# Splitting 576 output columns 512+64 (504+72) instead of 288+288 in a two-layer attention and MLP kernel

## The chip, the cores and the metric

The kernel runs on one core of one Trainium2 chip. The metric is the device time of one execution in microseconds (us), lower is better.

Engine names in the profile: PE is TensorE (matmul), PEld its weight loads, DVE is VectorE, ACT is ScalarE, POOL is GpSimd, and SPq is the queue of SyncE, from which most transfers and all DMA transposes are issued here. The granted clock is the share of TensorE's full clock that the chip's throttle let through, as the profiler recorded it.

## The reference, cut to what matters

The input is 2048 rows of D = 576 columns. Two layers, each an attention block and an MLP, both with a LayerNorm in front and a residual sum behind:

```python
x = x + A(layernorm(x), wqkv, wo)          # 32 heads of 18, sliding window of 256
x = x + B(layernorm(x), w1, b1, w2, b2)    # 576 -> 4608 -> gelu -> 576
x = x + A(layernorm(x), wqkv, wo)
x = x + B(layernorm(x), w1, b1, w2, b2)
```

Three kinds of matmul end in 576 columns: the projections to q, k and v, the output projection `wo`, and the second MLP matmul `w2`. Matmuls write to PSUM, which this kernel uses in banks; none of its matmuls is wider than 512 columns, and each output of 576 columns is made by two matmuls in two banks.

## The kernel before

The program is laid out by a planner at build time. The kernel describes tasks (one engine, what they read and write, an assumed cost and latency in us); the planner repeatedly takes the task that can start first by its assumed times, and so fixes for each engine one static order of instructions. The waits between engines are added afterwards. An assumed time can therefore be wrong without making the result wrong, but it decides what stands in front of what.

Rows are handled in chunks of 4 tiles of 128. While the attention of one chunk runs (scores on PE, exponentials on ACT, masks on POOL, then P times V on PE), PE fills its gaps with matmuls of the previous chunk's MLP and of the next chunk's projections.

```python
def mm_cost(n):                                   # what the planner assumes of a matmul, us
    return max(n / 2400.0, 0.026) + (0.006 if n > 64 else 0.0)

def two_out(lhs, rhs, n, reads, prio, after=()):  # projections and output projection
    bs = [Bank(FILL), Bank(FILL)]                 # FILL = (6, 5, 4): PSUM banks
    for o in range(2):
        ...                                       # 5 matmuls of n = 288 columns into bs[o]

# second MLP matmul: per tile two outputs, each 18 matmuls in three indivisible blocks of 6
for hh in range(2):
    b = Bank(FILL)
    for f0 in range(0, NFH, 6):                   # NFH = 18
        ...
        add("pe", fn, ..., cost=6 * mm_cost(HB))  # HB = 288
    resid(t, hh, b, prio, ...)                    # DVE: x_res += PSUM

# after the attention of a chunk: transpose its output by DMA, then the output projection
for i in range(nt):
    add("sp", lambda e, i=i: e.dma_start_transpose(attT[...], attq[:, i, :]),
        ..., dma="t", ring=8, cost=1.3, lat=4.0, move=0.6, prio=prio - 0.1)
```

The softmax here doesn't subtract the row's maximum and nothing guards it: scores larger than these inputs give would overflow.

## Time and profile before

| | before |
|---|---|
| time, median | 987.56 us (3 runs, 985.93 to 987.72) |
| PE busy share | 96% |
| DVE, ACT, POOL busy share | 32%, 59%, 37% |
| mean granted TensorE clock, profiled run | 0.991 |

From the page of the kernel before: the busy time of each engine with its share of the span, and the chain that ended last, by engine.

```profile
PE 949.5 (96%) x9592; PEld 606.9 (61%) x9592; DVE 317.1 (32%) x772; ACT 586.0 (59%) x705; POOL 368.8 (37%) x507
PE 78%; DMA 5%; DVE 5%; POOL 5%; ACT 4%; issue 3%; DVEq 0%; POOLq 0%
```

PE is the bound: whatever leaves it idle, or lengthens what it does, costs time.

From the groups of the same page: source line, engine, operation, shapes out<-in, count, then busy us and mean ns of one, then the engine's idle time just before and what ended it.

```profile
L776 PE MATMUL ps<-w_sb,hT 128*128 128x288 bf16 x2304 | 316.1, 288 | 6.0 <-DVE x_res L709 4.9
L751 PE MATMUL ps<-xnTm,w_sb 128*128 128x512 bf16 x1440 | 319.4, 379 | 0.1
L709 DVE TENSOR_TENSOR x_res<-ps,x_res 128x288 f32<-128x288 f32 x160 | 70.7, 449 | 363.4 <-PE ps L776 342.6
```

L776 is the second MLP matmul, L751 the first, L709 the eviction that adds the second one's result to the residual. The 288 ns of one matmul is not its price, since matmuls overlap. The price is the distance between starts, which the timeline gives (start us, length us, instructions of one kind merged):

```profile
954.73 12.25 PE L751 MATMUL ps<-xnTm,w_sb 128*128 128x512 bf16 x56
966.81 17.80 PE L776 MATMUL ps<-w_sb,hT 128*128 128x288 bf16 x144
```

So 512 columns cost (12.25 - 0.379)/55 = 215.8 ns and 288 columns cost (17.80 - 0.286)/143 = 122.5 ns.

L601 are transposes of q and k, L722 those of the attention output, L558 and L564 projections and output projection:

```profile
288.72 3.58 SPq L601 DMA_TRANSPOSE kT<-qn  x1
292.40 5.19 SPq L722 DMA_TRANSPOSE attT<-attq  x4
...
294.20 0.65 PE L558 MATMUL ps<-wqkv,xnTa 128*128 128x288 bf16 x4
294.69 0.29 PE L564 MATMUL ps<-wqkv,xnTa 128*128 128x288 bf16 x1
295.55 0.67 PE L558 MATMUL ps<-wo_sb,attT 128*128 128x288 bf16 x4 [0.57 <-DMA attT<-attq]
```

### The profile page before, as it was taken

The numbers are of one execution on the slowest core, as the hardware profiler recorded it, in microseconds if no ns is written. First come the engines' busy times: TensorE is split into PE (matmuls) and PEld (weight loads), VectorE is DVE, ScalarE is ACT, GpSimd is POOL, SyncE is SP. The second block draws the span as 40 slices with busy tenths as digits, with TensorE's granted clock in tenths as the row PEclk, the third lists the DMA queues.
The fourth block names the chain that finished last, engine by engine and source line by source line (L and its number), as shares of the span: only waits on it lengthen the run. The fifth ranks groups of instructions, "written<-read, shape, count | busy, mean of one in ns | idle before, by whom it ended". The sixth has DMA issues, their size and how long they took to land.

```text
span 987.9 us, 22924 instructions
## 1 busy us (share of the span) xinstructions
PE 949.5 (96%) x9592; PEld 606.9 (61%) x9592; DVE 317.1 (32%) x772; ACT 586.0 (59%) x705; POOL 368.8 (37%) x507
## 2 busy tenths in 40 slices
PE   8898889999999999999999999999999999999998
PEld 6665547655575656756476565756567564657556
DVE  5653612722145211534028130361115310132001
ACT  0476676377753777447761777627774487852531
POOL 4555725334333434325153252433333352531000
PEclk9999899999999999999999999999999999999999
DMA  9846380964269250881529542494516816084540
GB/s 195 173 116 136 74 253 15 208 174 138 68 145 192 60 178 28 188 187 34 191 56 204 136 126 80 133 170 106 169 49 167 177 44 198 14 220 118 172 132 25
DMA packets 227287, 129.58 MB, mean 131 GB/s; under 512 B 141808, under 2 KB 225008, under 8 KB 227184
## 3 DMA queue, kind: packets, MB, share of 16 engines
q1 hardware_dynamic: 217872, 120.43, 49.4%
q0 software_dynamic: 6880, 5.03, 2.7%
q10 hardware_dynamic: 2432, 2.65, 0.9%
q8 instruction: 76, 1.25, 0.5%
q14 instruction: 27, 0.22, 0.1%
HBM read 90.69 MB, written 2.36 MB: 94 GB/s over the span
## 4 chain that ended last, share of the span: by engine, by line
PE 78%; DMA 5%; DVE 5%; POOL 5%; ACT 4%; issue 3%; DVEq 0%; POOLq 0%
PE ps L776 29%; PE ps L751 27%; PE ps L558 7%; PE ps L675 7%; PE ps L628 6%; ACT pT L637 3%; POOL pT L658 2%; DMA attT<-attq 2%; DVE x_res L709 2%; PE ps L564 2%; POOL rstd L499 2%; DVE st_all L486 2%; DMA x_res<-in_A_x_dram 1%; DMA kT<-qn 1%; DVE xn L509 1%
## 5 line engine op out<-in xcount | busy, mean ns | idle before, releaser
L637 ACT ACTIVATE pT<-ps 128x1024 bf16<-128x1024 f32 (+2 forms) x384 | 347.2, 971 | 128.1 <-PE ps L628 126.9
L658 POOL TENSOR_SCALAR_AFFINE_SELECT pT<-pT 128x512 bf16<-128x512 bf16 (+1 forms) x368 | 278.1, 778 | 388.2 <-ACT pT L637 365.4
L755 ACT ACTIVATE hT<-ps,b1col 128x512 bf16<-128x512 f32 x288 | 196.5, 687 | 251.1 <-PE ps L751 250.8
L776 PE MATMUL ps<-w_sb,hT 128*128 128x288 bf16 x2304 | 316.1, 288 | 6.0 <-DVE x_res L709 4.9
L751 PE MATMUL ps<-xnTm,w_sb 128*128 128x512 bf16 x1440 | 319.4, 379 | 0.1
L776 PEld LDWEIGHTS ps<-w_sb,hT 128*128 128x128 bf16 x2304 | 211.2, 98 | 80.6 <-issue 20.2
L751 PEld LDWEIGHTS ps<-xnTm,w_sb 128*128 128x128 bf16 x1440 | 139.5, 98 | 159.6 <-issue 0.4
L709 DVE TENSOR_TENSOR x_res<-ps,x_res 128x288 f32<-128x288 f32 x160 | 70.7, 449 | 363.4 <-PE ps L776 342.6
L558 PE MATMUL ps<-wqkv,xnTa 128*128 128x288 bf16 x768 | 120.5, 286 | 8.9 <-DVE qn L594 5.0
L675 PEld LDWEIGHTS ps<-vA,pT 128*128 128x128 bf16 x2880 | 94.2, 96 | 29.2 <-issue 11.7
L675 PE MATMUL ps<-vA,pT 128*128 128x20 bf16 x2880 | 100.6, 172 | 5.6 <-DVE attq L690 2.7
L558 PEld LDWEIGHTS ps<-wqkv,xnTa 128*128 128x128 bf16 x768 | 71.2, 97 | 33.1 <-DVE qn L594 7.8
L628 PE MATMUL ps<-qT,kT 32*128 32x384 bf16 (+2 forms) x1408 | 75.0, 280 | 11.6 <-ACT pT L637 8.4
L594 DVE CAST qn<-ps 128x288 bf16<-128x288 f32 x128 | 57.4, 455 | 39.2 <-PE ps L564 38.3
L486 DVE BATCH_NORM_STATS2 st_all<-x_res 128x6 f32<-128x288 f32 x120 | 50.8, 446 | 17.2 <-DMA x_res<-in_A_x_dram 15.9
L509 DVE TENSOR_SCALAR xn<-x_res,mv_all,rstd 128x576 bf16<-128x576 f32 x60 | 47.2, 801 | 26.1 <-POOL rstd L499 14.6
L564 PE MATMUL ps<-wqkv,xnTa 128*128 128x288 bf16 x192 | 54.9, 286 | 0.0
L628 PEld LDWEIGHTS ps<-qT,kT 32*128 32x128 bf16 x1408 | 22.4, 92 | 49.0 <-issue 24.7
L733 POOL TENSOR_TENSOR x_res<-x_res,b2bc 128x576 f32<-128x576 f32 x32 | 45.2, 1415 | 13.7 <-DVE xn L509 12.9
L712 DVE TENSOR_TENSOR xn<-ps,x_res 128x288 bf16<-128x288 f32 x32 | 14.6, 458 | 110.9 <-PE ps L776 110.9
L497 POOL TENSOR_SCALAR vtmp<-mv_all 128x1 f32<-128x1 f32 (+1 forms) x43 | 8.6, 200 | 103.9 <-DVE mv_all L488 101.4
L685 DVE RECIPROCAL rinv<-ps 128x16 f32<-128x16 f32 x64 | 16.4, 257 | 95.7 <-PE ps L675 95.4
(32 smaller groups left out, 332.7 us busy)
## 6 DMA issues: line engine op xcount, KB each, us to landing
w_sb<-in_B_w_dram SPq DMA_DIRECT2D x144, 288.0 KB, 5.1
w_sb<-in_B_w_dram SPq DMA_DIRECT2D x72, 512.0 KB, 4.0
w_sb<-in_B_w_dram SPq DMA_DIRECT2D x72, 64.0 KB, 3.7
x_res<-in_A_x_dram POOLq DMA_DIRECT2D x4, 1152.0 KB, 7.0
out_dram<-xn SPq DMA_DIRECT2D x16, 144.0 KB, 1.8
wqkv<-in_A_wqkv_dram ACTq DMA_DIRECT2D x3, 576.0 KB, 5.9
hT<-in_A_x_dram SPq DMA_DIRECT2D x1, 576.0 KB, 5.2
wo_sb<-in_A_wo_dram ACTq DMA_DIRECT2D x1, 576.0 KB, 4.0
```

Of the source, the lines that this page charges most:

```text
L486: add("dve", lambda e, i=i, s=s: e.bn_stats(st_all[:, t, i, :], s[:, t, i * HB:(i + 1) * HB]), reads=res, writes=[f"st{t}_{i}"], cost=0.43 ...
L558: ins = e.matmul(bank(bs[o])[:, 0:n], lhs(o, c, full), rhs(o, c, full), start=(c == 0), stop=False)
L564: ins = e.matmul(bank(bs[o])[:, 0:n], lhs(o, 4, full), rhs(o, 4, full), start=False, stop=True)
L594: add("dve", lambda e, o=o, b=bs[o], qv=qv: e.tensor_copy(qv[:, o * 16:(o + 1) * 16, 0:DH], bank(b)[:, 0:HB].rearrange("p (h d) -> p h d", ...
L628: ins = e.matmul(two(bs[j // 2])[:, j % 2, col:col + nq * 128], kT[32 * j:32 * j + 32, g, (T0 + so) % KS, :], qT[32 * j:32 * j + 32, g, qo ...
L637: add("act", lambda e, h2=h2: e.activation(pT[:, sl, 2 * h2:2 * h2 + 2, lo:hi], two(bs[h2])[:, :, lo:hi], ACT.Exp, scale=SCALE), reads=[bs ...
L658: add("pool", lambda e, ap=ap, pat=pat, sgn=sgn, kind=kind: e.affine_select(ap, ap, pattern=pat, compare_op=(ALU.is_ge if kind == "d" else ...
L675: ins = e.matmul(bank(B_O)[:, o:o + VW], pT[:, sl, j, col + qi * 128:col + (qi + 1) * 128], vA[:, (T0 + so) % VS, 4 * g + j, :], start=(fi ...
L709: add("dve", lambda e: e.tensor_tensor(x_res[:, t, sl], bank(b)[:, 0:HB], x_res[:, t, sl], ALU.add), reads=[b], writes=[f"x{t}h{hh}"], cos ...
L751: ins = e.matmul(bank(bk)[:, 0:n], w1_sb[:, sl, col:col + 128], xnTm[:, k % 2, c, 0:n], start=(c == 0), stop=(c == KD - 1))
L755: add("act", lambda e, f=f, fl=fl, bk=bk: e.activation(hT[:, fl, 0:n], bank(bk)[:, 0:n], ACT.Gelu_apprx_tanh, bias=b1col[:, f:f + 1]), rea ...
L776: ins = e.matmul(bank(b)[:, 0:HB], hT[:, fl, i * 128:(i + 1) * 128], w2_sb[:, fl, hh * HB:(hh + 1) * HB], start=(fl == 0), stop=(fl == NFH ...
```

## The change

Its intent: a wide matmul carries the fixed cost of a matmul better, and the planner's cost function counts no fixed cost at all for 64 columns, so 512+64 looks cheaper to it than 288+288 (0.246 against 0.252 us). The projections are cut at a head's border, 504 = 28 heads of 18. The core of the diff (cut: an unused variant is deleted, the same substitutions recur, and two dependencies follow the new borders: the LayerNorm statistics of the second half wait for both outputs, and P times V waits for its head's part of V):

```diff
+    QS = (slice(0, 504), slice(504, 576))
+    DS = (slice(0, 512), slice(512, 576))
-            bs = two_out(... n * D + o * HB:n * D + (o + 1) * HB], HB, ...)
+            bs = two_out(... n * D + s.start:n * D + s.stop], QS, ...)
-   ... o * 16:(o + 1) * 16 ... bank(b)[:, 0:HB] ... cost=0.42
+   ... 28 * o:(28, 32)[o] ... bank(b)[:, 0:(504, 72)[o]] ... cost=(0.68, 0.2)[o]
-        sl = slice(hh * HB, (hh + 1) * HB)        # eviction: cost=0.46
+        sl = DS[hh]                               # cost=(0.74, 0.2)[hh]
-         lambda o, c, r: wo_sb[r, c, o * HB:(o + 1) * HB], HB, ...
+         lambda c, s: wo_sb[:, c, s], DS, ...
-  e.matmul(bank(b)[:, 0:HB], hT[...], w2_sb[:, fl, hh * HB:(hh + 1) * HB], ...)   cost=6 * mm_cost(HB)
+  e.matmul(bank(b)[:, 0:n],  hT[...], w2_sb[:, fl, DS[hh]], ...)                  cost=6 * mm_cost((512, 64)[hh])
```

More of the change, by code (lines that the diff above doesn't have):

```diff
@@ L331, in schedule @@
         return max(t.end for t in self.tasks)
-PAIR = False
-W1W = 2560
 WARM_UNTIL = 140.0
@@ L373, in build_kernel @@
     x_res = sb("x_res", [P, NT, D], FP32)
-    w1_sb = sb("w1_sb", [P, NB1, W1W], BF16)
+    w1_sb = sb("w1_sb", [P, NB1, 2560], BF16)
     w2_sb = sb("w2_sb", [P, NFH, D], BF16)
@@ L449, in build_kernel @@
     add("pool", lambda e: e.memset(nhalf[:, :], -0.5), writes=["nhalf"], cost=0.1, prio=-10)
-    if not PAIR:
-        add("pool", lambda e: e.memset(xn[:, :, D:KD * 128], 0.0), writes=[f"xn{i}" for i in range(NXN)], cost=0.4, prio=-10)
+    add("pool", lambda e: e.memset(xn[:, :, D:KD * 128], 0.0), writes=[f"xn{i}" for i in range(NXN)], cost=0.4, prio=-10)
     add("pool", lambda e: e.memset(vA[:, :, :, DH:VW], 1.0), writes=[f"v{s}h{h}" for s in range(VS) for h in range(2)], cost=1.6, prio=-8)
@@ L455, in build_kernel @@
             writes=[f"qn{i}h{h}" for h in range(2)], cost=0.5, prio=-9)
-    if not PAIR:
-        add("pool", lambda e: e.memset(attq[:, :, D:KD * 128], 0.0), writes=["aqd"], cost=0.5, prio=-8)
-        add("dve", lambda e: e.memset(wqkv[64:128, 4, :], 0.0), writes=["wqC", "wkC", "wvC"], cost=1.0, prio=-8)
-        add("dve", lambda e: e.memset(wo_sb[64:128, 4, :], 0.0), writes=["woC"], cost=0.4, prio=-8)
-        add("dve", lambda e: e.memset(w1_sb[64:128, :, 2048:2560], 0.0), writes=["w1Z"], cost=1.0, prio=-8)
+    add("pool", lambda e: e.memset(attq[:, :, D:KD * 128], 0.0), writes=["aqd"], cost=0.5, prio=-8)
+    add("dve", lambda e: e.memset(wqkv[64:128, 4, :], 0.0), writes=["wqC", "wkC", "wvC"], cost=1.0, prio=-8)
+    add("dve", lambda e: e.memset(wo_sb[64:128, 4, :], 0.0), writes=["woC"], cost=0.4, prio=-8)
+    add("dve", lambda e: e.memset(w1_sb[64:128, :, 2048:2560], 0.0), writes=["w1Z"], cost=1.0, prio=-8)
     dma("pool", b2bc[:, :], bass.AP(tensor=B_b2.tensor, offset=B_b2.offset, ap=[[0, P], [1, D]]), writes=["b2"], cls="b", ring=2,
@@ L483, in ln_stats @@
         for i in range(2):
-            res = [f"x{t}h{i}"] if srcres is None else [srcres]
+            res = X(t)[:i + 1] if srcres is None else [srcres]
             s = x_res if src is None else src
@@ L512, in ln_norm_T @@
         rd = [f"xn{sl}"]
-        if PAIR:
-            add("dve", lambda e: e.tensor_scalar(xn[:, sl, D:KD * 128], s[:, t, 512:D], mv_all[:, t, 0:1], rstd[:, t:t + 1],
-                                                  op0=ALU.subtract, op1=ALU.mult),
-                reads=res + [f"mv{t}", f"rstd{t}"], writes=[f"xd{sl}"], cost=0.12, prio=prio)
-            rd.append(f"xd{sl}")
         add("sp", lambda e: e.dma_start_transpose(dst[:, :, i * 128:(i + 1) * 128], xn[:, sl, :]),
@@ L533, in w1_load @@
             reads=reads, writes=[f"w1a{sl}"], cls="w1", cost=0.5, prio=prio)
-        if PAIR:
-            src = B_w1[512:576, cols].rearrange("p (a b f) -> p b a f", a=2, b=2)
-            for b in range(2):
-                dma("sp", w1_sb[64 * b:64 * b + 64, sl, 2048:2304].rearrange("p (a f) -> p a f", a=2), src[:, b],
-                    writes=[f"w1b{sl}_{b}"], cls="w1", cost=0.5, prio=prio)
-        else:
-            dma("sp", w1_sb[0:64, sl, 2048:2560], B_w1[512:576, cols], reads=["w1Z"], writes=[f"w1b{sl}_0"], cls="w1", cost=0.5,
-                prio=prio)
+        dma("sp", w1_sb[0:64, sl, 2048:2560], B_w1[512:576, cols], reads=["w1Z"], writes=[f"w1b{sl}_0"], cls="w1", cost=0.5, prio=prio)
     def w2_load(hf, prio, gate=False):
@@ L547, in w2_load, with two_out, fn @@
                 reads=[f"h{2 * pr}"] if gate else [], writes=[f"w2s{pr}"], cls="w2", ring=9, cost=0.6, prio=prio)
-    def two_out(lhs, rhs, n, reads, prio, after=()):
+    def two_out(lhs, rhs, cols, reads, prio, after=()):
         bs = [Bank(FILL), Bank(FILL)]
-        full = slice(0, 128)
         for o in range(2):
-            def fn(e, o=o):
+            n = cols[o].stop - cols[o].start
+            def fn(e, o=o, n=n):
                 ins = None
-                for c in range(4):
-                    ins = e.matmul(bank(bs[o])[:, 0:n], lhs(o, c, full), rhs(o, c, full), start=(c == 0), stop=False)
-                if PAIR and o == 1:
-                    for oo in range(2):
-                        r = slice(64 * oo, 64 * oo + 64)
-                        ins = e.matmul(bank(bs[oo])[:, 0:n], lhs(oo, 4, r), rhs(oo, 4, r), start=False, stop=True, tile_position=(64 * oo, 0))
-                if not PAIR:
-                    ins = e.matmul(bank(bs[o])[:, 0:n], lhs(o, 4, full), rhs(o, 4, full), start=False, stop=True)
-                return ins
-            w = [bs[0], bs[1]] if (o == 1 and PAIR) else [bs[o]]
-            cost = mm_cost(n) * (4 if PAIR else 5) + (mm_cost(n) * 1.2 if PAIR and o == 1 else 0.0)
-            add("pe", fn, reads=reads, writes=w, cost=cost, prio=prio, alloc=((bs if o == 0 else ()) if PAIR else [bs[o]]), after=after)
+                for c in range(KD):
+                    ins = e.matmul(bank(bs[o])[:, 0:n], lhs(c), rhs(c, cols[o]), start=(c == 0), stop=(c == KD - 1))
+                return ins
+            add("pe", fn, reads=reads, writes=[bs[o]], cost=mm_cost(n) * KD, prio=prio, alloc=[bs[o]], after=after)
         return bs
@@ L579, in qkv @@
             dest = [f"v{A % VS}h{o}" for o in range(2)] if w == "v" else [f"qn{qn_ctr[0] % NQN}h{o}" for o in range(2)]
-            bs = two_out(lambda o, c, r: xnTa[r, c, i * 128:(i + 1) * 128],
-                         lambda o, c, r, n=n: wqkv[r, c, n * D + o * HB:n * D + (o + 1) * HB], HB,
+            bs = two_out(lambda c: xnTa[:, c, i * 128:(i + 1) * 128],
+                         lambda c, s, n=n: wqkv[:, c, n * D + s.start:n * D + s.stop], QS,
                          [f"w{w}A", f"w{w}B", f"w{w}C", f"xa{i}"], prio + 0.01 * n, after=dest)
@@ L585, in qkv @@
                 for o in range(2):
-                    add("dve", lambda e, o=o, b=bs[o]: e.tensor_copy(vA[:, sv, o * 16:(o + 1) * 16, 0:DH],
-                                                                   bank(b)[:, 0:HB].rearrange("p (h d) -> p h d", d=DH)),
-                        reads=[bs[o]], writes=[f"v{sv}h{o}"], cost=0.42, prio=prio)
+                    add("dve", lambda e, o=o, b=bs[o]: e.tensor_copy(vA[:, sv, 28 * o:(28, 32)[o], 0:DH],
+                                                                   bank(b)[:, 0:(504, 72)[o]].rearrange("p (h d) -> p h d", d=DH)),
+                        reads=[bs[o]], writes=[f"v{sv}h{o}"], cost=(0.68, 0.2)[o], prio=prio)
             else:
@@ L593, in qkv @@
                 for o in range(2):
-                    add("dve", lambda e, o=o, b=bs[o], qv=qv: e.tensor_copy(qv[:, o * 16:(o + 1) * 16, 0:DH],
-                                                                          bank(b)[:, 0:HB].rearrange("p (h d) -> p h d", d=DH)),
-                        reads=[bs[o]], writes=[f"qn{sl}h{o}"], cost=0.42, prio=prio)
+                    add("dve", lambda e, o=o, b=bs[o], qv=qv: e.tensor_copy(qv[:, 28 * o:(28, 32)[o], 0:DH],
+                                                                          bank(b)[:, 0:(504, 72)[o]].rearrange("p (h d) -> p h d", d=DH)),
+                        reads=[bs[o]], writes=[f"qn{sl}h{o}"], cost=(0.68, 0.2)[o], prio=prio)
                 if w == "q":
@@ L679, in fn @@
             return ins
-        rd = [f"p{sl}h0", f"p{sl}h1"] + [f"p{sl}m{i}" for i in range(3)] + [f"v{(T0 + p[0]) % VS}h{g // 4}" for p in parts]
+        rd = [f"p{sl}h0", f"p{sl}h1"] + [f"p{sl}m{i}" for i in range(3)] + [f"v{(T0 + p[0]) % VS}h{g // 7}" for p in parts]
         add("pe", fn, reads=rd, writes=[f"pb{B_O}"], cost=0.026 * 4 * sum(p[2] for p in parts), prio=prio, lat=0.2)
@@ L705, in resid @@
     def resid(t, hh, b, prio, outp=None):
-        src = bank
-        sl = slice(hh * HB, (hh + 1) * HB)
+        sl = DS[hh]
+        n = sl.stop - sl.start
         if outp is None:
-            add("dve", lambda e: e.tensor_tensor(x_res[:, t, sl], bank(b)[:, 0:HB], x_res[:, t, sl], ALU.add),
-                reads=[b], writes=[f"x{t}h{hh}"], cost=0.46, prio=prio)
-        else:
-            add("dve", lambda e: e.tensor_tensor(xn[:, outp, sl], bank(b)[:, 0:HB], x_res[:, t, sl], ALU.add),
-                reads=[b, f"x{t}h{hh}"], writes=[f"xn{outp}" if hh == 0 else f"xd{outp}"], cost=0.46, prio=prio)
+            add("dve", lambda e: e.tensor_tensor(x_res[:, t, sl], bank(b)[:, 0:n], x_res[:, t, sl], ALU.add),
+                reads=[b], writes=[f"x{t}h{hh}"], cost=(0.74, 0.2)[hh], prio=prio)
+        else:
+            add("dve", lambda e: e.tensor_tensor(xn[:, outp, sl], bank(b)[:, 0:n], x_res[:, t, sl], ALU.add),
+                reads=[b, f"x{t}h{hh}"], writes=[f"xn{outp}" if hh == 0 else f"xd{outp}"], cost=(0.74, 0.2)[hh], prio=prio)
     def tail(k, prio):
@@ L717, in tail @@
         rd = [f"aq{g}" for g in range(G)]
-        if PAIR:
-            add("dve", lambda e: e.tensor_copy(attq[:, 0:nt, D:KD * 128], attq[:, 0:nt, 512:D]), reads=rd, writes=["aqd"], cost=0.25,
-                prio=prio)
         for i in range(nt):
@@ L725, in tail @@
             t = t0 + i
-            bs = two_out(lambda o, c, r, i=i: attT[r, c, i * 128:(i + 1) * 128],
-                         lambda o, c, r: wo_sb[r, c, o * HB:(o + 1) * HB], HB, [f"aT{i}", "woA", "woB", "woC"], prio)
+            bs = two_out(lambda c, i=i: attT[:, c, i * 128:(i + 1) * 128], lambda c, s: wo_sb[:, c, s], DS,
+                         [f"aT{i}", "woA", "woB", "woC"], prio)
             for o in range(2):
@@ L774, in fn @@
                         ins = None
+                        n = DS[hh].stop - DS[hh].start
                         for fl in range(f0, f0 + 6):
-                            ins = e.matmul(bank(b)[:, 0:HB], hT[:, fl, i * 128:(i + 1) * 128], w2_sb[:, fl, hh * HB:(hh + 1) * HB],
+                            ins = e.matmul(bank(b)[:, 0:n], hT[:, fl, i * 128:(i + 1) * 128], w2_sb[:, fl, DS[hh]],
                                            start=(fl == 0), stop=(fl == NFH - 1))
@@ L779, in mm2 @@
                     add("pe", fn, reads=[f"h{fl}" for fl in range(f0, f0 + 6)] + [f"w2s{fl // 2}" for fl in range(f0, f0 + 6)], writes=[b],
-                        cost=6 * mm_cost(HB), prio=prio + 0.05 * i, alloc=((b,) if f0 == 0 else ()))
+                        cost=6 * mm_cost((512, 64)[hh]), prio=prio + 0.05 * i, alloc=((b,) if f0 == 0 else ()))
                 resid(t, hh, b, prio, outp=(osl if fin else None))
```

## The prediction

> What bounds the kernel now. TensorE. In the busy table PE is busy 949.5 of 987.9 us (96%) and PE holds 78% of the chain that ended last; DVE (32%), ACT (59%) and POOL (37%) have slack. The slices show PE at 9 tenths from slice 9 on. What matters on PE is the distance from one matmul's start to the next, not the 286 ns of one matmul. The timeline gives it: 144 matmuls of 288 columns took 17.80 us at the end of the kernel, so (17.80-0.286)/143 = 122.5 ns; 56 of 512 columns took 12.25 us, so 215.8 ns; bursts of 16 with 20 columns took 0.55 us, so 25 ns, each with its own weight load. The Trainium skill, "TensorE: Matmul & The Clock Gate", section "Wait - 56ns, not 53.3ns?", gives N/2.4 + 2.5 ns and a floor near 25 ns; the trace agrees at all three sizes. Weight loads (98 ns each) overlap and cost no distance of their own, since 25 ns was reached with one per matmul.
>
> What the change does. Every pair of outputs keeps its count: 1152 pairs in the second MLP matmul, 480 in the projections, 160 in the output projection, 1792 together. No instruction is added or removed there; only widths move. A pair costs 2 x 122.5 = 245 ns now; after, 215.8 + about 29 (64 columns, estimate from the formula) = 245 ns, and 504+72 gives 212.5 + 32.5 = 245 ns. The array has the same 576 columns to stream and the per-matmul cost of about 2.5 ns stays: the saving is nil, within +-2 us over 1792 pairs.
>
> DVE. An eviction of 288 columns takes 449 ns (groups view). With one fp32 element per cycle at 0.96 GHz (Trainium skill, "Trainium Kernel Development and Optimization", section "NeuronCore Architecture") about 150 ns of it are fixed, so I estimate 680 ns for 512 and 215 for 64 (680 and 230 for 504 and 72): the sum, about 0.9 us a pair, stays.
>
> What is left is order. PE waits for evictions: in the groups and waits views 6.0 us before the second MLP matmul, 8.9 us before the projections; the gaps of 0.72 us (second MLP matmul with one free bank) and about 1.2 us (projections) recur in each chunk, some 20 us in all. A wide bank is held longer, a narrow one shorter; the longer first run may cover some waits for the exponentials, while the wider eviction lengthens its own wait. The static order of the whole program is recomputed, so these gaps move; I expect -8 to +6 us net. Each LayerNorm chain after the output projection starts its statistics about 0.3 us later, exposed only in the first chunk. The last eviction is about 0.23 us shorter, on the critical path.
>
> Prediction: 985 us, 80% range 973 to 998. Faster by over 2%: 0.05; within 2%: 0.90; slower by over 2%: 0.05.
>
> What would show it. Right: distances near 216 and 29 ns in the second MLP matmul, the last 144 matmuls again about 17.6 us; DVE busy within 3% of 317 us; PE busy share 95 to 97%; the difference found in waits for DVE x_res, DVE qn and ACT pT. Wrong: the 64-column matmuls start 40 ns or more apart (consecutive ones accumulate into the same 64 columns, which the 20-column bursts do not): each 10 ns more costs 18 us over 1792 pairs. Also wrong if PE waits for evictions double, or if the granted clock drops for longer in the first 155 us, where now three stretches run at half clock; or if the new order fills the attention stages much better, which could save over 10 us.

## More of the kernel before

From the view of waits of the kernel before (who waited for what: us in total, times, longest):

```profile
ACT pT L637 <- PE ps L628: 126.9, 107, 27.8
PEld ps L558 <- DMA attT<-attq: 3.1, 4, 0.9
PE ps L558 <- DMA attT<-attq: 1.8, 4, 0.6
```

ACT waits 126.9 us in all for scores, and PE's matmul records show 1.8 us of waiting for the transposed attention output `attT`.

The profiler records every instruction of one execution; its matmul records can be incomplete by about a per cent.

## The result, and the profile after

The changed kernel takes 998.4 us (median of 6 runs, 995.61 to 1005.78), the kernel before 986.43 us in the pooled runs. The ratio is 1.0134, with a 95% interval of 1.0096 to 1.0173. Ratios here and below are the mean time of one kernel's fast runs over that of the other's of the same rounds, so not quite the ratio of the medians that are quoted. The change is inside the 2% band, but it is a clear loss of about 12 us. The runs also spread over 10 us, where those of the kernel before spread over 2.5 us. All outputs are right.

First, what did not change. The page's busy line and chain after:

```profile
PE 941.7 (95%) x9424; PEld 487.0 (49%) x9552; DVE 309.7 (31%) x772; ACT 586.7 (59%) x705; POOL 370.0 (37%) x507
PE 80%; DMA 6%; POOL 4%; DVE 4%; issue 3%; SPq 2%; ACT 1%; POOLq 0%; DVEq 0%
```

The trace has 9552 weight loads but only 9424 matmuls, so 128 matmul records are missing and PE's busy time is read a little low. (Before there were 9592: the new plan has 240 warm-up matmuls in the first 140 us instead of 280. That is not the loss, since e6 below has 238 and is fast.) The groups by shape (now L753 is the second MLP matmul, L688 its eviction) and the timeline of the last matmuls:

```profile
L688 DVE TENSOR_TENSOR x_res<-ps,x_res 128x512 f32<-128x512 f32 x80 | 54.8, 685 | 307.2 <-PE ps L753 252.0 <-PE ps L545 54.9
L688 DVE TENSOR_TENSOR x_res<-ps,x_res 128x64 f32<-128x64 f32 x80 | 16.9, 212 | 16.1 <-PE ps L753 15.7
...
975.23 17.80 PE L753 MATMUL ps<-w_sb,hT 128*128 128x512 bf16 x142
```

The evictions cost 685 + 212 = 897 ns a pair, against 2 x 449 = 898. The last 144 matmuls (two records missing, both widths merged in this line) take 17.80 us, exactly as before. In the whole trace the median distance between starts is 216 ns at 512 columns, 213 at 504, 32 at 72 and 29 at 64. The change is neutral in PE's and DVE's own work.

What did change is in the waits:

```profile
ACT pT L616 <- PE ps L607: 167.4, 125, 27.3
PEld ps L545 <- DMA attT<-attq: 15.6, 9, 3.5
PE ps L545 <- DMA attT<-attq: 11.5, 7, 3.0
```

ACT waits 40 us longer for scores, and PE waits 11.5 us for `attT` instead of 1.8. The end of the same chunk's attention as shown before (L580: q and k transposes, L698: attention output, L727: first MLP matmul):

```profile
301.09 1.28 SPq L580 DMA_TRANSPOSE kT<-qn  x1
302.46 1.24 SPq L698 DMA_TRANSPOSE attT<-attq  x1
303.79 1.09 SPq L430 DMA_DIRECT2D w_sb<-in_B_w_dram  x2
304.93 4.66 SPq L698 DMA_TRANSPOSE attT<-attq  x3
...
299.17 1.39 PE L545 MATMUL ps<-wqkv,xnTa 128*128 128x504 bf16 x10
300.39 4.48 PE L727 MATMUL ps<-xnTm,w_sb 128*128 128x512 bf16 x20
305.15 1.40 PE L545 MATMUL ps<-wo_sb,attT 128*128 128x512 bf16 x10 [0.28 <-DMA attT<-attq]
306.39 1.24 PE L727 MATMUL ps<-xnTm,w_sb 128*128 128x512 bf16 x5
310.25 4.07 PE L545 MATMUL ps<-wo_sb,attT 128*128 128x512 bf16 x19 [2.62 <-DMA attT<-attq]
```

PE does not have less work to cover the transposes than before: 1.39 and 4.48 us of projections and first-MLP matmuls stand before the output projection. It is the transposes that come late. SPq takes its entries in order, about 1.3 us each. Before, one transpose of k stood in front of `attT`; now q and k transposes fill the queue until 302.37, although this chunk's attention had ended at 297.8, and two weight loads stand between the first `attT` and the other three. So the last leaves the queue only at 309.6, and PE stands still for 2.62 us. Over the five chunks of the middle of the program (all but the first of each layer and the last), the first `attT` is issued 4.6 us after the end of its attention, against 2.0 us before; four or five q and k transposes stand in front of it, where there were one or two. The view by stretches (from:to in us, busy us of each engine with its count, then granted clock, DMA share, GB/s) shows what follows. The first line is the kernel before over the end of its own transposes, the others are the changed kernel:

```profile
290.00:296.00 6.00, 5.43 (x45) 4.11 (x44) 4.12 (x9) 0.00 (x0) 0.00 (x0) 1.00 0.82 178
...
304.00:310.00 6.00, 3.35 (x20) 1.24 (x17) 1.76 (x5) 1.89 (x3) 0.73 (x2) 1.00 1.08 177
310.00:314.00 4.00, 3.75 (x14) 1.63 (x16) 1.91 (x5) 0.00 (x0) 0.65 (x1) 0.57 0.83 179
314.00:320.00 6.00, 5.95 (x37) 2.91 (x37) 5.07 (x16) 2.15 (x4) 3.99 (x7) 1.00 0.67 150
```

Just after the standstill the granted clock is 0.57 over 4 us: a stretch of 3.4 us at half clock. The same follows the 2.99 us wait at 187 us, but none follows the 2.67 us wait at 776.6 (the section on the clock, below, shows why). In the timed runs the mean granted clock is 0.986 to 0.990 (6 runs), against 0.991 to 0.997 for the kernel before (11 runs of the next rounds).

The account of the profiled pair (996.2 against 987.9 us, 8.3 us apart): adding up all gaps over 0.12 us between PE's matmul records, and the time after the last one, gives 45.6 us idle after and 37.8 before, 7.8 us more. Gaps that end in an output projection are 12.8 us after and 1.8 before. So the wait for `attT` is more than the whole growth of PE's idle time; other gaps shrank by about 3 us. This pair understates the clock, since the profiled run of the kernel before had one of the lowest clocks of all its runs, 0.991. Within the span it has 17.1 us at half clock, all in the first 152 us, and the changed kernel 23.9: 13.7 in that first part and 10.2 later, where the kernel before has none. Of these, 3.4 us follow each of two waits for `attT`, and 3.4 fall at the end of the second layer's attention. The section on the account by the clock, below, uses all the timed runs.

### The profile page after: what moved, and what is told of

The parts are those of the page before. It is cut to its first block, busy times and chain, and to the rows that moved or that the text cites. A ratio compares the mean times of both kernels' runs of the same rounds, so it can differ in the third digit from the quotient of the medians.

```text
span 996.2 us, 22673 instructions
## 1 busy us (share of the span) xinstructions
PE 941.7 (95%) x9424; PEld 487.0 (49%) x9552; DVE 309.7 (31%) x772; ACT 586.7 (59%) x705; POOL 370.0 (37%) x507
## 4 chain that ended last, share of the span: by engine, by line
PE 80%; DMA 6%; POOL 4%; DVE 4%; issue 3%; SPq 2%; ACT 1%; POOLq 0%; DVEq 0%
PE ps L753 29%; PE ps L727 28%; PE ps L545 13%; PE ps L654 6%; PE ps L607 4%; POOL pT L637 3%; DMA attT<-attq 2%; DMA x_res<-in_A_x_dram 2%; DVE x_res L688 1%; ACT pT L616 1%; DVE st_all L484 1%; SPq L580 1%; DVE qn L573 1%; POOL rstd L497 1%; DMA xnTa<-xn 1%
## 5 line engine op out<-in xcount | busy, mean ns | idle before, releaser
L727 PE MATMUL ps<-xnTm,w_sb 128*128 128x512 bf16 x1393 | 316.0, 380 | 3.3 <-issue 1.1
L753 PE MATMUL ps<-w_sb,hT 128*128 128x512 bf16 (+1 forms) x2231 | 299.5, 284 | 11.5 <-DVE x_res L688 6.0
L727 PEld LDWEIGHTS ps<-xnTm,w_sb 128*128 128x128 bf16 x1440 | 137.1, 98 | 157.9 <-issue 1.5
L753 PEld LDWEIGHTS ps<-w_sb,hT 128*128 128x128 bf16 x2304 | 138.0, 98 | 132.6 <-issue 15.1
L688 DVE TENSOR_TENSOR x_res<-ps,x_res 128x512 f32<-128x512 f32 (+1 forms) x160 | 70.2, 448 | 323.3 <-PE ps L753 267.7
L545 PE MATMUL ps<-wqkv,xnTa 128*128 128x504 bf16 (+1 forms) x960 | 135.4, 289 | 7.6 <-DVE qn L573 3.4
L545 PEld LDWEIGHTS ps<-wqkv,xnTa 128*128 128x128 bf16 x960 | 61.6, 99 | 65.2 <-DVE qn L573 8.3
L573 DVE CAST qn<-ps 128x504 bf16<-128x504 f32 (+1 forms) x128 | 54.5, 452 | 58.2 <-PE ps L545 54.2
L545 PE MATMUL ps<-wo_sb,attT 128*128 128x64 bf16 (+1 forms) x312 | 45.1, 297 | 12.9 <-DMA attT<-attq 11.5
L507 DVE TENSOR_SCALAR xn<-x_res,mv_all,rstd 128x576 bf16<-128x576 f32 x60 | 45.1, 761 | 36.7 <-DMA xnTm<-xn 19.3
L545 PEld LDWEIGHTS ps<-wo_sb,attT 128*128 128x128 bf16 x320 | 22.9, 102 | 38.4 <-DMA attT<-attq 15.6
```

The costliest lines, as they stand in the source:

```text
L545: ins = e.matmul(bank(bs[o])[:, 0:n], lhs(c), rhs(c, cols[o]), start=(c == 0), stop=(c == KD - 1))
L573: add("dve", lambda e, o=o, b=bs[o], qv=qv: e.tensor_copy(qv[:, 28 * o:(28, 32)[o], 0:DH], bank(b)[:, 0:(504, 72)[o]].rearrange("p (h d) - ...
L688: add("dve", lambda e: e.tensor_tensor(x_res[:, t, sl], bank(b)[:, 0:n], x_res[:, t, sl], ALU.add), reads=[b], writes=[f"x{t}h{hh}"], cost ...
L727: ins = e.matmul(bank(bk)[:, 0:n], w1_sb[:, sl, col:col + 128], xnTm[:, k % 2, c, 0:n], start=(c == 0), stop=(c == KD - 1))
L753: ins = e.matmul(bank(b)[:, 0:n], hT[:, fl, i * 128:(i + 1) * 128], w2_sb[:, fl, DS[hh]], start=(fl == 0), stop=(fl == NFH - 1))
```

## The experiments

Two theories at first. Order theory: the loss comes from the new static order, above all from where the output projection stands against `attT`. Width theory: it comes from the wide and narrow instructions themselves. Since the planner's assumed costs are separate from the instructions, the two can be crossed exactly. Each run has 5 rounds, on the same chip as the kernel before.

### Widths and order crossed (e1, e2)

e1: the changed kernel, planner told the old costs. All instructions of all engines stand in the positions of the kernel before.

```diff
-  cost=mm_cost(n) * KD              -  cost=(0.68, 0.2)[o]   -  cost=(0.74, 0.2)[hh]   -  cost=6 * mm_cost((512, 64)[hh])
+  cost=mm_cost(288) * KD            +  cost=0.42             +  cost=0.46              +  cost=6 * mm_cost(288)
```

> The changed kernel (504+72 and 512+64 columns), but its static planner is told the costs of the kernel before; every engine then has its instructions in exactly the order of the kernel before (checked position by position), only the widths differ. Order theory (the loss comes from the new static order, above all from the output projection placed where the transposed attention output has not landed): 984 to 989 us, ratio to before 0.998 to 1.003, PE idle time waiting for the attT transposes back to about 3 us, spread of the runs under 3 us. Width theory (the loss comes from the wide and narrow instructions themselves, their evictions and the bank held longer): about 998 us, ratio about 1.012.

Measured: 1039.23 us, ratio 1.0526 (1.0505 to 1.0547). From its waits:

```profile
PEld ps L607 <- ACT pT L616: 36.5, 53, 1.9
PE ps L607 <- ACT pT L616: 29.5, 43, 1.8
```

e2 is the mirror: all widths 288, planner told the new costs, so exactly the order of the changed kernel.

```diff
-  cost = mm_cost(n) * ...   -  cost=0.42               -  cost=0.46                -  cost=6 * mm_cost(HB)
+  cost = mm_cost(cols[o]) * 5   +  cost=(0.68, 0.2)[o]     +  cost=(0.74, 0.2)[hh]     +  cost=6 * mm_cost((512, 64)[hh])
```

> The mirror: all outputs 288+288 as in the kernel before, but the planner is told the costs of the changed kernel, so every engine has exactly the order of the changed kernel. Order theory: about 996 to 1000 us, ratio 1.010 to 1.014, PE waiting some 10 us for the attT transposes, runs spread over 5 us or more. Width theory: about 986 us, ratio 1.00.

Measured: 1010.55 us, ratio 1.0222 (1.0196 to 1.0247), with 9.8 us of PE's matmuls waiting for `attT`.

| | planned as 288+288 | planned as 512+64 |
|---|---|---|
| run as 288+288 | 987.62 (before) | 1010.55 (e2) |
| run as 512+64 | 1039.23 (e1) | 998.4 (after; earlier rounds) |

Both theories fall in their plain form. Neither the widths nor the order has a price of its own: each order suits the widths it was planned for, and the two mismatches end 23 and 52 us above the kernel before. In e1 PE runs into scores whose PSUM banks ACT has not emptied (29.5 us against 8.4 us in the kernel before), probably because a slot meant for 0.73 us of MLP matmuls holds 0.17 or 1.30 us (argued, not tested). The `attT` wait goes with the order: gone in e1, back in e2.

### The wait for the transposes (e3), and a control (e4)

```diff
-  add("sp", ... dma_start_transpose(attT[...]) ..., lat=4.0, ...)
+  add("sp", ... dma_start_transpose(attT[...]) ..., lat=9.0, ...)
```

> The changed kernel with one number changed in the planner: the attT transposes are assumed to take 9.0 us after their issue instead of 4.0, so that the output projection is placed about 4 us later in PE's order (behind 8.6 us of first-MLP matmuls instead of 4.3). If the wait for attT is the loss: PE's idle time before the output projection falls from about 11 us to under 3 us and the time to 986 to 991 us. If that wait only hides another limit: the wait goes but the time stays within 3 us of 998.

Measured: 989.71 us (984.79 to 994.2), ratio 1.002 (0.9991 to 1.0048). In the waits view `attT` no longer appears for PE. ACT's wait for scores stays high, at 171.2 us. One number in the planner takes away the loss, though not all of the spread. ACT's longer wait alone does not cost it, then. But e3 is not a clean removal of the `attT` wait: SPq's entries around `attT` stand as in the changed kernel and the output projection comes later (11.6 us after the end of the attention instead of 7.8), and in about a fifth of PE's positions (2067 of 9552) another kind of matmul stands. e16 and e17 below touch the queue alone.

e4 is the kernel before with another matmul cost, `max(n / 2400, 0.0225) + 0.0025`, in the planner.

> Control: the kernel before with its widths, but the planner's matmul cost changed a little (N/2.4 + 2.5 ns, as measured, instead of N/2.4 + 6 ns), which changes about a fifth of PE's positions but keeps the projections ahead of the output projection. If any change of order costs, 992 us or more; if only the placing of the output projection against attT does, 983 to 989 us.

Measured: 983.2 us, ratio 0.995 (0.9935 to 0.9966). A change of order as such does not cost; this one gains 4 us.

### Which part of the change (e5, e6)

e5 splits the second MLP matmul only; projections and output projection stay 288+288 with their costs.

```diff
-    QS = (slice(0, 504), slice(504, 576))
+    QS = (slice(0, 288), slice(288, 576))
+    WS = (slice(0, 288), slice(288, 576))      # output projection; DS stays 512+64 for the second MLP matmul
```

> Only the second MLP matmul is split 512+64; projections and output projection stay 288+288. The planner is told the matching costs. In its order the projections move forward into the attention part and the output projection stands behind 4.3 to 6.5 us of first-MLP matmuls, as in the changed kernel. If that shift of the projections is what costs: 992 to 1000 us with PE waiting 5 us or more for attT. If the projections' own split costs: 986 to 989 us.

Measured: 998.31 us, ratio 1.0099 (1.0083 to 1.0115). Its waits:

```profile
ACT pT L617 <- PE ps L608: 165.6, 132, 29.0
PE ps L546 <- DMA attT<-attq: 13.9, 11, 3.2
```

e6 splits the projections only (`DS` set to 288+288, its costs to match).

```diff
-    DS = (slice(0, 512), slice(512, 576))
+    DS = (slice(0, 288), slice(288, 576))
```

> Only the q, k, v projections are split 504+72; second MLP matmul and output projection stay 288+288, costs to match. In its order about 7.3 us of projections still stand directly before the output projection, as in the kernel before. If the shift caused by the MLP split is the cost: 985 to 990 us and little wait for attT. If the projections' own split costs: 993 us or more.

Measured: 982.6 us, ratio 0.9947 (0.9928 to 0.9966), faster than its expected range; ACT's wait for scores is 124.6 us and PE's for `attT` 1.9 us. The loss belongs to the MLP split. The split of the projections gains 5 us; no run here says by what, and e4's gain of the same size shows that a small shift of order can do it.

### Both widths under a corrected plan (e7, e8)

Both get the planner's matmul cost as measured and 9.0 us for `attT`; e7 has the new widths, e8 the old ones.

```diff
-        return max(n / 2400.0, 0.026) + (0.006 if n > 64 else 0.0)
+        return max(n / 2400.0, 0.0225) + 0.0025
-  lat=4.0
+  lat=9.0
```

> The changed kernel's widths with both planner corrections: matmul cost N/2.4 + 2.5 ns for every width (the changed kernel's planner gives 64 columns no fixed cost and 512 columns 6 ns) and 9.0 us for the attT transposes. If widths do not matter once the plan fits them: equal to the next run within 3 us, 982 to 988 us. If the coarse and fine blocks stay worse fillers in the attention part: 3 to 10 us slower than the next run.

> The kernel before's widths with the same two planner corrections as the run before this one. Expected 980 to 985 us: the measured matmul cost alone gave 983.2 us; the wait for attT that is left there is about 1 us, so the later output projection gains 0 to 2 us or loses as much by a later LayerNorm.

Measured: 986.88 us (ratio 0.9986) and 982.71 us (ratio 0.9949). With an honest plan, 512+64 is still 4 us slower than 288+288. ACT's wait for scores is 164.6 us in e7 and 128.2 us in e8. It is over 160 us in every run so far whose widths or plan have the MLP split (e1 and e2 too: 164.2 and 182.8), and 124 to 129 us in the others. By the account further below most of the 4 us between e7 and e8 is clock: 8.6 against 5.4 us lost to it, with remainders of 978.1 and 977.4 us.

### Why the MLP split shifts the order: the blocks (e9, e10, e13, e14)

Third theory: the planner can only place whole blocks of 6 matmuls. A block of 1.30 us between two attention steps makes ACT wait for scores. The rest of the attention is then planned later, and projections are drawn in among it that used to stand behind it, with their q and k transposes, which so come to stand in front of `attT`. The rival: a wide output holds its PSUM bank longer, whatever the blocks. e9 keeps the widths, the planner's numbers and the banks, and changes the blocks:

```diff
-                for f0 in range(0, NFH, 6):
+                BL = (3, 18)[hh]                # wide half 3 x 216 = 0.65 us, narrow half 18 x 29 = 0.53 us
+                for f0 in range(0, NFH, BL):
```

> The changed kernel, widths and planner numbers kept, but the planner may cut the second MLP matmul's wide half after every 3 matmuls (0.65 us) instead of 6 (1.30 us), and gives the narrow half as one block of 18 (0.53 us) instead of three of 0.17 us; before the change all blocks were 0.73 us. Block theory (uneven filler blocks between the attention steps keep the exponentials waiting): ACT's wait for scores falls from 167 us towards 127 us, and the time to 985 to 992 us. Bank theory (a wide output holds its PSUM bank longer, whatever the blocks): ACT's wait stays above 155 us and the time above 994 us, unless the wait for attT happens to shrink because the projections stand later in this order.

Measured: 981.73 us (980.17 to 984.55), ratio 0.9944 (0.9928 to 0.9961): the full change, now faster than the kernel before. Its waits:

```profile
ACT pT L616 <- PE ps L607: 153.9, 124, 27.1
PEld ps L545 <- DMA attT<-attq: 8.1, 7, 2.0
PE ps L545 <- DMA attT<-attq: 5.4, 7, 1.9
```

The time fell more than expected, ACT's wait less (153.9, where 127 was hoped for). The attention of the chunk shown above ends at 288.7 us, as in the kernel before (289.0), and not at 297.8. The queue in front of `attT` is only partly mended: no weight load stands between the four of this chunk any more, and over the five middle chunks the first is issued 3.4 us after the end of the attention (2.0 before, 4.6 in the changed kernel).

e10 goes the other way: the kernel before, 288+288, with blocks of 9 (1.10 us).

```diff
-                for f0 in range(0, NFH, 6):
+                BL = (9, 9)[hh]
+                for f0 in range(0, NFH, BL):
```

> The kernel before with its widths, but the second MLP matmul in blocks of 9 (1.10 us) instead of 6 (0.73 us). Block theory: ACT's wait for scores rises from 127 us to 140 us or more and the time to 990 us or more. Bank theory: ACT's wait stays within 8 us of 127 and the time within 4 us of 987.

Measured: 990.98 us, ratio 1.0039 (1.0023 to 1.0055). Its waits:

```profile
ACT pT L637 <- PE ps L628: 142.5, 101, 28.0
PE ps L558 <- DMA attT<-attq: 7.9, 7, 2.5
```

Both are as the block theory expected. Coarser blocks alone, with the old widths, bring part of the same symptoms: ACT's wait up by 16 us, `attT` from 1.8 to 7.9 us, the time up by 4 to 5 us.

e9 changed both halves. e13 cuts only the wide half (`BL = (3, 6)[hh]`), e14 joins only the narrow one (`BL = (6, 18)[hh]`).

> One half of the run with the wide half in threes: wide half in blocks of 3 (0.65 us), narrow half in three blocks of 6 (0.17 us each) as in the changed kernel. If the coarse wide block is the cause: 980 to 986 us and ACT's wait for scores near 154 us. If the many tiny narrow blocks are the cause: 994 us or more.

> The other half: wide half in blocks of 6 (1.30 us) as in the changed kernel, narrow half as one block of 18 (0.53 us). If the coarse wide block is the cause: still 994 to 1000 us, PE waiting about 10 us for attT. If the tiny narrow blocks are: 980 to 988 us.

Measured: e13 986.4 us (ratio 0.9987, 0.9964 to 1.0009), just over the expected range; e14 999.05 us (ratio 1.0121, 1.0096 to 1.0145). ACT's wait is 155.9 us in e13; in e14 PE waits 9.4 us for `attT`. The coarse wide block sets the loss off: e14 leaves it and loses as much as the change. It does so only under this plan, for e3 and e7 keep it and lose little once the planner assumes 9.0 us for `attT`. Joining the narrow half is worth about 4 us more once the wide half is fine (ratio 0.9944 against 0.9987, in different rounds and on another chip), and nothing by itself.

### Looking for the best version (e11, e12, e15)

e11 is e6 with the matmul cost of e4; e12 adds `lat=6.0`; e15 is e9 with `lat=6.0`.

> Candidate for the best: only the projections split 504+72 (982.6 us alone), with the planner's matmul cost N/2.4 + 2.5 ns (983.2 us alone on the kernel before). If both gains are of one kind (the order before the output projection) they do not add: 980 to 984 us. If they add: 976 to 979 us.

> As the run before this one, with 6.0 us instead of 4.0 us assumed for the attT transposes. Expected 978 to 983 us: about 2 us of waiting for attT is left in the projections-only kernel, and a later output projection delays the LayerNorm behind it.

> The full change with the wide half in threes, the narrow half whole, and 6.0 us instead of 4.0 us assumed for the attT transposes. The wait for attT that is left there (5.4 us before the matmul records in the waits view) should fall under 2 us and the time to 977 to 981 us; if 982 us or more, that wait was no longer on the critical path.

Measured: e11 980.53 us (ratio 0.9942, 0.9923 to 0.996), e12 983.05 us (0.9963), just over its range, e15 983.14 us (0.996). e15 missed its range: PE no longer waits for `attT`, yet the time is no better than e9's, so the 5.4 us left there did not cost by themselves. The gains of e4 and e6 did not add. e9 and e11 both beat the kernel before by about 0.6%, and their intervals overlap; none of the versions gets clearly below 980 us.

### The queue alone (e16, e17)

If `attT` is late because of what stands before it in SPq, moving those entries must take the wait away with everything else untouched. e16 takes the finished plan of the changed kernel and moves, in each chunk, the q and k transposes directly before the first `attT` transpose behind the fourth. e17 moves the two weight loads between the four as well. PE, DVE, ACT and POOL keep every position; only about 50 of SPq's 465 positions change.

```diff
         order = sorted(order + extra, key=lambda x: x[0])
+        seq = [t for _, t in order]
+        # for each chunk, for each q/k transpose t directly before its first attT transpose, last one first:
+            if any(id(s) in successors_of_t for s in seq[at + 1:to + 1]):   # to: the fourth attT transpose
+                break
+            seq.pop(at); seq.insert(to, t)
```

> The changed kernel with the order of every engine but the DMA queue kept position by position; in the DMA queue, the 4 or 5 transposes of q and k that stand directly before the attention output's transposes are moved behind them (six chunks). If the queue makes attT late: PE's wait for attT falls from 11.5 us to 5 us or less and the time to 985 to 992 us. If attT is late for another reason (attention ends late, slow landings): 995 us or more and the wait stays.

> As the run before this one, and the two weight loads that stand between the four transposes of the attention output are moved behind the fourth. If the queue is all of it: PE's wait for attT under 2 us and 983 to 989 us; the loads for the first MLP matmul come some 3 us later, which should not matter.

Measured: e16 995.98 us (989.16 to 1000.71), ratio 1.0082 (1.0052 to 1.0112); e17 995.68 us (990.79 to 1001.55), ratio 1.0077 (1.0049 to 1.0105). From the waits of the changed kernel (first line) and of e16:

```profile
DVE xn L507 <- DMA xnTm<-xn: 19.3, 11, 3.7
...
DVE xn L524 <- DMA xnTm<-xn: 34.9, 14, 5.2
PE ps L770 <- DVE x_res L705: 7.3, 15, 1.0
PE ps L562 <- DVE qn L590: 5.5, 7, 3.3
PE ps L562 <- DMA attT<-attq: 2.1, 1, 2.1
```

The wait for `attT` falls from 11.5 to 2.1 us (1.9 in e17), and the first `attT` is issued as soon as the attention ends. So the order of the queue made it late: that is shown. But both runs missed their ranges by 4 us and more: only about 0.5 of the 1.3% comes back.

The two runs are not a clean removal either. What was moved behind `attT` now stands before the LayerNorm transposes (`xnTm`) of the same queue, and DVE's wait for these rises from 19.3 us to 34.9 (e16) and 37.6 (e17). DVE's evictions stand behind that wait in its order, and PE waits for them: 3.26 us at 532.9 in e16, and 2.27, 2.06, 3.62 and 2.43 us at 209.0, 327.5, 540.5 and 682.5 in e17. A stretch at half clock begins towards the end of each of these five waits or within 2 us after it. In the changed kernel the longest wait of that kind after the first 150 us is 1.72 us. So part of the queue's delay was passed on, and how much of the loss the queue makes in all stays open.

### The account by the clock

Here the mean granted clock of every timed run helps. At half clock a stretch of d us does d/2 of work, so time x (1 - clock) is the time lost to the throttle if PE would have been busy throughout; it is an upper bound, worked out for each run and averaged. The clock is recorded to three digits, which leaves half a us open in each run. The remainder is about what the same run would take at full clock, an estimate. The rows come from different chips; the kernel before lost 4.2 to 4.9 us and kept a remainder of 981.9 to 983.2.

| | mean time | lost to the clock | remainder |
|---|---|---|---|
| before (11 runs) | 987.6 | 4.5 | 983.2 |
| after | 999.8 | 12.3 | 987.5 |
| e16, e17 (queue mended) | 995.0, 995.4 | 13.3, 13.3 | 981.7, 982.1 |
| e2 (old widths, order of the change) | 1009.7 | 9.9 | 999.8 |
| e3 (output projection later) | 989.8 | 11.7 | 978.1 |
| e14 (wide block coarse) | 998.6 | 11.0 | 987.6 |
| e13 (wide block fine) | 985.6 | 9.2 | 976.4 |
| e9 (both blocks right) | 982.0 | 6.2 | 975.7 |
| e6 (projections only) | 982.8 | 8.4 | 974.5 |

By this account the change's 12 us are about 4 us at full clock, standstill above all, and about 8 us of clock. With the attention transposes first in the queue (e16, e17) the first part is gone, the remainder being at or just under that of the kernel before, and the second is not smaller. The half clock does not come from the waits for `attT` alone, as the profile had suggested: e3 has none of them in its waits view and runs at the same low clock. e16 and e17 do not decide this, since they have other long waits. Fine blocks lower the remainder by 11 us, in e13 as in e9, and bring the clock part down from 12.3 us to 9.2 (e13) and 6.2 (e9). The widths are not needed for it: e2, with 288+288 throughout, has 9.9 us of it.

The profiles, one for each of the 19 kernels, show when the clock falls. Apart from the last stretch at half clock, which the end of the record cuts, all last 3.41 or 6.83 us and start on a grid of 3.41 us that is fixed within a run: in the changed kernel 190.90, 310.36 and 873.56 us are 35 and 165 steps apart. Of the steps at full clock, all 35 in which PE was busy less than 42% of the time were followed by half clock, and none with more than 76%; in between both occur. (Gaps up to 0.12 us count as busy.) So it matters where a wait lies. The 2.62 us at 307.6 fall into one step, in which PE was 23% busy. The 2.67 us at 776.6 are cut by a grid line at 778.0, with PE about 61% busy in either step, and the clock stayed full.

Besides the long waits there is a second place, the end of the second layer's attention. Three lines of PE and a stretch of the changed kernel, then PE in the kernel before:

```profile
871.48 0.56 PE L654 MATMUL ps<-vA,pT 128*128 128x20 bf16 x16 [0.69 <-POOL pT L637]
873.75 0.61 PE L607 MATMUL ps<-qT,kT 32*128 32x256 bf16 x8 [1.34 <-ACT pT L616]
874.59 0.60 PE L654 MATMUL ps<-vA,pT 128*128 128x20 bf16 x16 [0.23 <-POOL pT L637]
873.56:876.97 3.41, 2.76 (x28) 1.30 (x30) 0.00 (x0) 3.39 (x5) 3.12 (x4) 0.50 0.99 316
...
866.63 0.40 PE L628 MATMUL ps<-qT,kT 32*128 32x256 bf16 x8 [0.29 <-ACT pT L637]
```

Between these last attention steps PE has no MLP matmul left to fill with. In the last 75 us of that attention all 11 kernels planned for the 512+64 split of the MLP (after, e2, e3, e5, e7, e9, e13 to e17) have two gaps of 1.34 us and 3.4 to 10.2 us at half clock, which is 1.7 to 5.1 us lost. The seven with 288+288 there in plan and widths (before, e4, e6, e8, e10, e11, e12) have no gap over 0.77 us and no half clock there; e1, of mixed kind, has gaps up to 0.98 us and 3.4 us of it. This part of the clock loss goes with the MLP split, with fine blocks too. It is read from the profiles; no run isolates it.

## Why the prediction was wrong, point by point

- **PE is the bound.** Right: 96% before and 95% after.
- **A pair costs the same on PE (245 ns both ways).** Right, to the nanosecond: 216 + 29 = 245 and 213 + 32 = 245, and the last 144 matmuls take 17.80 us in both. The prediction leaned on the Trainium skill, "TensorE: Matmul & The Clock Gate", section "Wait — 56ns, not 53.3ns?", and this trace agrees at 64, 72, 504 and 512 columns. The feared extra distance of consecutive narrow matmuls into the same columns did not show.
- **A pair costs the same on DVE.** Right: 897 ns against 898; estimated were 680 and 215, measured 685 and 212. The section that the prediction cites gives the 0.96 GHz; the one element per cycle is not in it, but this trace bears it out: (685 - 212)/448 = 1.06 ns a column, where 1/0.96 is 1.04.
- **"The longer first run may cover some waits for the exponentials."** In the changed kernel's own plan PE's waits for exponentials did fall, from 8.4 to 5.9 us before the scores. The other direction was missed: ACT's wait for scores rose by 40 us.
- **"The static order of the whole program is recomputed, so these gaps move; I expect -8 to +6 us net."** This is the step that failed. The term was named but sized from the old gaps alone (evictions and exponentials), and these moved little: PE's waits for `x_res` went from 4.9 to 6.0 us, for `qn` from 5.0 to 3.4. The term measured +12 us. By the account above, an estimate, about 4 us came from standstill, above all from a wait that was 1.8 us before, that of the output projection for the DMA transposes of the attention output, 11.5 us in the matmul records. About 8 us came from a lower granted clock, which the prediction named only as a risk for the first 155 us; in the profiled pair that part has less half clock than before (13.7 against 17.1 us), and the new half clock lies behind it. The links, and what shows each: the wide block doubled in length because the count of 6 was kept, and that sets off the loss (e9 and e13 take it away with the same widths, e14 does not, e10 brings part of it with the old ones; e3 shows that a later output projection avoids most of it too); projections, and with them q and k transposes, move forward into the attention (read from the orders); these transposes stand before `attT` in the in-order queue and make it late (e16 and e17).
- **The range.** 973 to 998 missed the median of 998.4 by 0.4 us. The 0.90 for "within 2%" held.

What stays open: how the 8 us of clock divide. The profiles show them after long waits of PE and at the end of the second layer's attention, but no run isolates either. By the timed runs they do not simply go with the coarse wide blocks: e6 and e13 have 8.4 and 9.2 us without them. Also open is why ACT's wait remains at 154 us with fine blocks while it is 127 us with 288+288, and where the gain of the projections' split comes from. That the planner draws the projections forward because of the later scores is read from the orders; only its trigger, the block, and its end, the queue, were tested.

## What to carry to other kernels

Where one engine's gaps are filled with another stage's work, a change of a tile's width is also a change of the filler's grain: keep the time of an indivisible block, not its count of instructions. If a planner or a hand-made order rests on assumed latencies, look also at what stands before each urgent transfer in its in-order queue, and, when you move it forward, at what you push back. Split the time of every run by its granted clock before crediting a wait with the whole of a loss. Cross widths and order as in e1 and e2 before blaming either.

## What the Trainium skill lacked or had wrong

- "TensorE: Matmul & The Clock Gate", section "Back-to-back issue gap", gives about 131 ns per matmul at 512 columns for a stream of weight load and matmul pairs. Here such a stream runs at 215.8 ns (56 matmuls in 12.25 us), which is that page's figure for the isolated gap.
- The same page, section "Why this matters for your kernels", warns of PE gaps over about 3 us. Here shorter gaps are enough: a half-clock stretch of 3.4 us follows a gap of 2.62 us (none follows one of 2.67 us that a line of the 3.41 us grid cuts), and at the end of the second layer's attention one follows two gaps of 0.69 and 1.34 us with little PE work between them (changed kernel, 870.8 to 873.8 us).
- "DMA: Bandwidth & Descriptors", section "DMA Transpose (X-bar)", gives no time from issue to landing. Here a 128x640 bf16 transpose in SBUF takes 2.6 to 6.2 us to land (median 3.6 us in the changed kernel) next to other transfers, and about 1.3 us of the issuing queue each.
- "Perfetto Trace Analysis", section "Matmuls", says that larger matmuls are more efficient than smaller ones when possible. By the column that holds here, if slightly: 0.42 ns at 512 columns (215.8 ns), 0.45 at 64 (29 ns). But 512+64 and 288+288, with as many matmuls, cost the same 245 ns, and as filler between attention steps the large ones came with a loss of 12 us until their blocks were cut finer. No page speaks of the grain of filler work.
